# Shifted value blocks of streaming heads: built by SBUF-to-SBUF transfers on SyncE's queue instead of GpSimd copies, from the fourth chunk on

## The chip, the core and the metric

The kernel runs on one core of a Trainium2 chip. The core has five engines, each with its own in-order queue of instructions: TensorE (PE in the profile, its weight loads PEld), VectorE (DVE), ScalarE (ACT), GpSimd (POOL) and SyncE (SP). SyncE does no arithmetic here; it only begins transfers. Sixteen DMA engines move the data of all transfers, whoever begins them. The metric is the time of one execution on the device in microseconds (us), less being better; the time given for a kernel is the median of its runs.

## What is computed

Attention with two kinds of heads, followed by a gated feed-forward block. Four batches, 8 heads, 768 positions, 64 values per head. "Retrieval" heads (0, 2 and 6) see every earlier position; the other five, the "streaming" heads, see a window of the last 64 positions and the first 4 positions, the sinks.

```python
stream_keep = causal & (is_sink | in_win)      # is_sink: pos < 4, in_win: rel < 64
mask = np.where(retr[0, :, 0, 0, None, None], full_mask, stream_mask)
scores = np.where(mask[None, :, :, :], scores, -1000000000.0)
a = np.exp(scores - max)  ;  a = a / sum(a)
attn = np.matmul(a, v)
...
h = x @ w_in                                   # x: attn as 3072 x 512, w_in: 512 x 2048
g = h * (1.0 / (1.0 + np.exp(-beta * h)))
return (g @ w_out)                             # w_out: 2048 x 512
```

## The kernel before

**Units and chunks.** Each half sequence (384 positions, three blocks of 128) of a batch is a chunk; there are eight, c0 to c7, in the order (batch 0, first half), (1, first), (0, second), (1, second), (2, first), (3, first), (2, second), (3, second). A chunk has four units, one per pair of heads: heads (0, 2), (1, 3), (4, 6), (5, 7). So the first unit of a chunk has no streaming head, and the second has two. Units 0 to 7 (c0, c1) run in a hand-written start, `RAMP`. From unit 8 on, a loop with one turn `t` per unit (line 833) lays the scores of unit t, the value products of unit t-1 and slices of the feed-forward block of earlier chunks beside each other, in the order of a hand-written row of `PLAN`.

**Values.** `load_v` (line 124) brings a block of values from HBM by SP's queue into `vs`; `cast_v` (line 248) converts it to bf16 in `VX`, a buffer for each parity of the batch with six blocks of 128 positions by 8 heads by 65 numbers (64 values and a one, which makes the row sum). From c4 on GpSimd does this cast, for c2 and c3 VectorE.

**Shifted blocks.** A streaming head multiplies, for a block of queries, the block of keys before it as a whole. The first 64 of its 128 rows are outside every window, so rows 0 to 3 of that block are given to the sinks. The keys so rebuilt are `KO`, the values `VO`: four blocks per batch parity, copies of `VX` blocks 1 to 4 whose rows 0 to 3 are rows 0 to 3 of `VX` block 0. `sink_values(c)` (line 253) builds them: one block in a first half, three in a second half, a copy of 128 partitions by 512 numbers for each and then one copy on 4 partitions for the sink rows. All of it runs on GpSimd. `values_at` (line 265) calls it right behind the chunk's third `cast_v`.

**What follows from VO.** Value products (`steps_PV`, line 515) accumulate in PSUM in `po`; `normalize` (line 538) divides by the sum into `x`; `x_by_dma` (line 558) turns two units' `x` into half of `xT` by a DMA transpose on SP's queue. The feed-forward block of a chunk (line 600, then 653) needs both halves of its `xT`: of the four products of a 128-column slice, the first two read the half of the first two units, the third and fourth the other half.

**Other users of the queues.** GpSimd also begins the loads of rows of queries and keys from HBM (`load_rows`, line 276, 12 for each chunk). SP begins, besides `vs` and `xT`, the DMA transposes of those rows into `KT` and `QTD` (lines 294 and 297, six for each chunk) and the stores of results (line 659).

**What sets the order.** `later(delay, fn)` (line 73) keeps a function until a modelled clock, which each step of PE advances by its listed cost, has passed the time plus `delay`, or until someone who needs it calls it. Everything is issued in this order into the engines' queues, and dependencies between engines become semaphore waits.

```python
    def values_at(c, t, delay):
        def go():
            cast_v(c, t, nc.vector.tensor_copy if c < 4 else nc.gpsimd.tensor_copy)
            if t == HT - 1:
                sink_values(c)
        chunk_values.setdefault(c, []).append(later(delay, go))
```

Of the kernel before, what the change touches and what calls it, by code (L numbers as in the profile page):

```python
# [18 lines left out]
def kernel(  # L19
# [13 lines left out]
    nc = tc.nc  # L33
# [6 lines left out]
    HT = HALF // 128  # L40
    NPAIR = H // 2
    NU = B * 2 * NPAIR
# [3 lines left out]
    n_sink_i = 4  # L46
# [26 lines left out]
    def later(delay, fn):  # L73

        todo = [fn]

        def once():
            if todo:
                todo.pop()()
        heapq.heappush(heap, (clock[0] + delay, count[0], once))  # L80
        count[0] += 1
        return once
# [40 lines left out]
    def load_v(c, held=False, tiles=range(HT)):  # L123
        b, h2 = chunks[c]
        if tiles[0] == 0:
            staged["v", c] = stage.tile([128, HT, H, D], F32, name="vs")
        vs = staged["v", c]
        if held:
            nc.gpsimd.memset(vs[:, :, 0, 0:1], 0.0)
        for t in tiles:  # L130
            r = h2 * HALF + t * 128
            nc.sync.dma_start(out=vs[:, t], in_=v[b, :, r:r + 128, :].rearrange("h p d -> p h d"))  # L132
# [115 lines left out]
    def cast_v(c, t, copy):  # L248

        b, h2 = chunks[c]  # L250
        copy(out=VX[b % 2][:, h2 * HT + t, :, 0:D], in_=staged["v", c][:, t])  # L251

    def sink_values(c):
        b, h2 = chunks[c]
        ka, kz = (1, 2) if h2 == 0 else (2, 5)
        vx, vo = VX[b % 2], VO[b % 2]
        copy = nc.gpsimd.tensor_copy if c < 2 else nc.gpsimd.tensor_copy
        for i in range(ka, kz):
            copy(out=vo[:, i - 1, :, 0:D], in_=vx[:, i, :, 0:D])  # L259
        copy(out=vo[0:n_sink_i, ka - 1:kz - 1, :, 0:D],  # L260
             in_=vx[0:n_sink_i, 0:1, :, 0:D].to_broadcast([n_sink_i, kz - ka, H, D]))

    chunk_values = {2: []}

    def values_at(c, t, delay):
        def go():
            cast_v(c, t, nc.vector.tensor_copy if c < 4 else nc.gpsimd.tensor_copy)
            if t == HT - 1:
                sink_values(c)
        chunk_values.setdefault(c, []).append(later(delay, go))  # L270

    def sinks_at(u, delay):
        st_u[u]["sinks"] = later(delay, lambda: sinks_of(u))


    def load_rows(c):

        b, h2 = chunks[c]

        def rows(name, src, t, i):  # L280
            r = h2 * HALF + t * 128
            nc.gpsimd.dma_start(out=ROWS[c % 2, name][:, t, i * 4 * D:(i + 1) * 4 * D].rearrange("p (h d) -> p h d", d=D),  # L282
                                in_=src[b, i:H:2, r:r + 128, :].rearrange("h p d -> p h d"))
        return [lambda name=name, src=src, t=t, i=i: rows(name, src, t, i)
                for name, src in (("k", k), ("q", q)) for t in range(HT) for i in range(2)]

    def transposes_dma(c, names=("k", "q")):
        b, h2 = chunks[c]
        kr, qr = ROWS[c % 2, "k"], ROWS[c % 2, "q"]
        QT = QTD[(c + 1) % 2]  # L290
        for t in range(HT):
            j = h2 * HALF + t * 128
            if "k" in names:
                nc.sync.dma_start_transpose(out=KTB[b % 2][:, :, j:j + 128], in_=kr[:, t])
        for t in range(HT):
            if "q" in names:
                nc.sync.dma_start_transpose(out=QT[:, :, t * 128:(t + 1) * 128], in_=qr[:, t])
        for u in range(c * NPAIR, (c + 1) * NPAIR):
            p = u % NPAIR
            st_u[u] = {"QT": QT[:, place[p], :]}  # L300
# [34 lines left out]
    def steps_T(u):  # L335
        def go():
            transpose_qk(u, "k")
            transpose_qk(u, "q")
            copy_qk(u, "k", nc.vector.tensor_copy)
            copy_qk(u, "q", nc.scalar.copy)  # L340
            st_u[u]["sinks"] = later(600, lambda: sinks_of(u))
        return [(350, go)]
# [172 lines left out]
    def steps_PV(u):  # L515
        b, h2, p = units[u]
        s = st_u.setdefault(u, {})

        def head(hh, qi, last):
            def go():  # L520
                for f in s["masks"] + chunk_values[u // NPAIR] if u >= 8 else []:
                    f()
                if "po" not in s:
                    if u < 8 and u % 2:
                        po = ps_m.tile([128, 512], F32, name="mm")
                        s["po"] = po[:, 0:HT * 2 * (D + 1)].rearrange("p (t h d) -> p t h d", t=HT, h=2)
                    else:
                        s["po"] = sums_bank(u)[:, 0:HT * 2 * (D + 1)].rearrange("p (t h d) -> p t h d", t=HT, h=2)
                po = s["po"]
                lst = s["blocks"][hh][qi]  # L530
                for j, (e, val) in enumerate(lst):
                    nc.tensor.matmul(po[:, qi, hh, :], e, val, start=(j == 0), stop=(j == len(lst) - 1))  # L532
                if last and u >= 8:
                    normalize(u)
            return (len(s["blocks"][hh][qi]) * 38, go)
        return [head(hh, qi, hh == 1 and qi == HT - 1) for qi in range(HT) for hh in range(2)]
# [26 lines left out]
    def steps_X(g):  # L563

        def go():
            src = xg.pop(g)
            tp = ps_m.tile([128, 512], F32, name="mm").bitcast(BF16)[:, 0:2 * HALF].rearrange("p (a t j) -> p a t j", a=2, t=HT)
            for a in range(2):
                for t in range(HT):
                    nc.tensor.transpose(tp[:, a, t, :], src[:, a, t].rearrange("p h d -> p (h d)"), ident)  # L570
            x_tp[g] = tp
            if g >= 4:
                copy_x(g, nc.vector.tensor_copy)
        return [(340, go)]
# [111 lines left out]
    def run(steps):  # L686
        for x in steps:
            step(x)
# [8 lines left out]
    def do(word):  # L697
# [15 lines left out]
        elif what == "cv":  # L713
            cast_v(n, i, copies[eng])
        elif what == "vo":
            sink_values(n)
        elif what == "pv":
            pv = products.setdefault(n, [])
# [51 lines left out]
    def feed(x):  # L770

        a = done[0] < len(first) and all((first[done[0]][0], p) in avail for p in range(2))
        b = done[1] < len(second) and done[0] >= due[second[done[1]][0]]
        c = first[done[0]][0] if a else 0
        fresh = c > 1 and clock[0] < since[c] + 1300
        if b and (x == "b" or not a or fresh):
            done[1] += 1
            step(second[done[1] - 1][1])
        elif a:
            wide[0] = x == "A"  # L780
            done[0] += 1
            step(first[done[0] - 1][1])
            wide[0] = False
# [49 lines left out]
    for t in range(8, NU + 2):  # L833
        c, i = (t + 5) // NPAIR, (t + 5) % NPAIR
        if t >= 14 and c < NCHUNK and i < 3:
            for x, f in enumerate(load_rows(c)[4 * i:4 * i + 4]):
                later(1000 + 1500 * x, f)
        c, i = (t + 4) // NPAIR, (t + 4) % NPAIR
        if t >= 12 and c < NCHUNK and i < HT:
            later(2500, lambda c=c, i=i: load_v(c, tiles=[i]))  # L840
        c, i = (t + 3) // NPAIR, (t + 3) % NPAIR
        if t >= 9 and c < NCHUNK and i < HT:
            values_at(c, i, 3000)
        if t > 14 and t % NPAIR == 2 and t // NPAIR + 1 < NCHUNK:
            transposes_dma(t // NPAIR + 1)
        if 12 <= t + 1 < NU:
            sinks_at(t + 1, 1000)
        qk = steps_QK(t) if t < NU else []
        pv = steps_PV(t - 1) if 8 <= t - 1 < NU else []
        xx = steps_X(5) if t == 13 else steps_X(NU // 2 - 1) if t == NU + 1 else []  # L850
        tr = steps_T(t + 1) if t + 1 < 12 else []

        plan = PLAN[t - 8]
        for x in plan.split():
            if x == "V":
                run(qk[:1])
                qk = qk[1:]
            elif x == "p":
                run(pv[:1])
                pv = pv[1:]  # L860
            elif x == "T":
                run(tr)
                tr = []
            elif x == "X":
                run(xx)
                xx = []
            elif len(x) > 1:
                do(x)
            else:
                feed(x)  # L870
        run(qk + tr + xx + pv)
    i = 0
# [39 lines left out]
```

## Time and profile before

| | |
|---|---|
| time, median of 3 runs | 228.94 us (228.17 to 230.06) |
| time of the profiled execution | 228.94 us |
| its span, first to last instruction | 227.0 us |
| granted TensorE clock | 0.999 |
| VO copies on GpSimd, whole blocks (line 259) | 16, median 0.627 us |
| VO copies on GpSimd, sink rows (line 260) | 8, 0.607 to 1.679 us |
| value products that read VO (line 532) | 80 |
| share of the 16 DMA engines, 60 to 200 us: SP's queue (q1), GpSimd's queue (q0) | 52.4%, 41.6% |

The span is what the trace covers; the execution's time is 1.94 us longer. A row of a group of instructions reads: line, engine, operation, what is written and read, shape, count, then busy microseconds and mean nanoseconds of one, then the idle time of the engine before them and what ended it. A timeline row reads: start, duration, engine, line, operation, tiles, count, and the idle time before in brackets. For SP ("SPq") a row is the time in which the queue issues a transfer, not the transfer itself; how long that takes to land is told in the view of the transfers. On GpSimd the issue of a transfer is an instruction of its own (DMA_DIRECT2D, about 0.75 us).

### The profile page before, as it was taken

The page shows a single profiled execution, that of the slowest core. Times are in us where ns is not written, and L with a number is a line of the kernel's source. Part 1 is how long each engine was busy: PE and PEld are TensorE (multiplying, and loading weights), DVE is VectorE, ACT ScalarE, POOL GpSimd, SP SyncE. Part 2 cuts the span into 40 slices and gives each one's busy share as a digit, 9 for nine tenths or more (in the row PEclk, how much of TensorE's full clock was granted, in tenths as well). Part 3 has the DMA queues.
Part 4 walks back from the last instruction along what each step waited for, and adds up shares of the span by engine and source line. Part 5 has one row for each costly group of instructions (what it writes and reads, how often), then busy time and mean ns, then how long its engine had stood idle before and what let it go on. Part 6 is the DMA issues. An engine that isn't in the chain of part 4 may idle for free.

```text
span 227.0 us, 5019 instructions
## 1 busy us (share of the span) xinstructions
PE 219.4 (97%) x1898; PEld 126.4 (56%) x1917; DVE 142.1 (63%) x342; ACT 154.0 (68%) x254; POOL 87.3 (38%) x143
## 2 busy tenths in 40 slices
PE   7989999999999999999999999999999999999994
PEld 3555766654655665556654664556645655456553
DVE  4679888852684779357932699646963779028600
ACT  2698898946767897449933887569876878139621
POOL 5377952249163399143064049910670000000000
PEclk9999999999999999999999999999999999999999
DMA  6999999999999899989869779596963030111012
GB/s 204 262 301 239 225 197 198 195 220 171 149 216 178 161 153 144 141 175 133 103 131 162 126 151 140 92 133 103 216 64 107 24 81 0 49 46 46 0 49 92
DMA packets 95383, 31.66 MB, mean 139 GB/s; under 512 B 81776, under 2 KB 92416, under 8 KB 95360
## 3 DMA queue, kind: packets, MB, share of 16 engines
q1 hardware_dynamic: 58880, 22.82, 50.2%
q0 software_dynamic: 35904, 8.13, 41.9%
q10 hardware_dynamic: 576, 0.40, 0.6%
q8 instruction: 15, 0.25, 0.5%
q14 instruction: 8, 0.07, 0.1%
HBM read 27.27 MB, written 6.29 MB: 148 GB/s over the span
## 4 chain that ended last, share of the span: by engine, by line
PE 89%; DMA 4%; DVE 2%; SPq 2%; issue 1%; ACT 0%; ACTq 0%; DVEq 0%
PE mm L653 34%; PE mm L600 25%; PE sp L600 12%; PE sp L451 6%; PE po L532 6%; DMA s<-in_k_dram 3%; DMA s<-in_q_dram 2%; PE mm L638 2%; DVE es L478 1%; PE mm L322 1%; SPq L132 1%; PE mm L570 1%; PE mm L451 1%; SPq L119 1%; PE sp L422 1%
## 5 line engine op out<-in xcount | busy, mean ns | idle before, releaser
L653 PE MATMUL mm<-w_out_sb,gT 128*128 128x512 bf16 x349 | 84.1, 379 | 1.3 <-issue 0.5
L460 ACT ACTIVATE es<-sp 128x768 bf16<-128x768 f32 (+2 forms) x72 | 56.5, 837 | 19.6 <-PE sp L451 19.4
L600 PE MATMUL mm<-xT,w_in_sb 128*128 128x384 bf16 x348 | 64.6, 326 | 0.0
L600 PEld LDWEIGHTS <-w_in_sb 128*128 128x128 bf16 x512 | 47.8, 98 | 29.7 <-issue 0.2
L605 ACT ACTIVATE th<-mm,beta_h 128x384 f32<-128x384 f32 x87 | 49.8, 588 | 5.6 <-PE mm L600 0.9
L653 PEld LDWEIGHTS <-gT 128*128 128x128 bf16 x368 | 33.4, 98 | 36.0 <-issue 1.5
L608 DVE SCALAR_TENSOR_TENSOR gT<-th,mm 128x384 bf16<-128x384 f32 x87 | 46.8, 551 | 7.4 <-ACT th L605 3.8
L282 POOL DMA_DIRECT2D s<-in_q_dram x30 | 22.4, 761 | 27.2 <-DMA QTD<-s 21.7
L600 PE MATMUL sp<-xT,w_in_sb 128*128 128x384 bf16 x164 | 32.3, 326 | 0.0
L657 ACT ACTIVATE osb<-mm 128x512 f32<-128x512 f32 x23 | 13.8, 602 | 26.1 <-PE mm L653 25.8
L532 PEld LDWEIGHTS <-es 128*128 128x128 bf16 x472 | 23.3, 98 | 13.6 <-issue 1.5
L608 DVE SCALAR_TENSOR_TENSOR gT<-th,sp 128x384 bf16<-128x384 f32 x41 | 22.3, 552 | 5.6 <-ACT th L605 3.7
L532 PE MATMUL po<-VX,es 128*128 128x65 bf16 x360 | 24.9, 194 | 0.8 <-ACT VX L251 0.4
L605 ACT ACTIVATE th<-sp,beta_h 128x384 f32<-128x384 f32 x41 | 23.8, 586 | 2.3 <-PE sp L600 0.2
L282 POOL DMA_DIRECT2D s<-in_k_dram x30 | 22.4, 759 | 6.8 <-DMA w_out_sb<-in_moe_w_out_dram 5.2
L251 POOL CAST VX<-vs 128x512 bf16<-128x512 f32 x16 | 10.6, 662 | 34.6 <-DMA vs<-in_v_dram 31.8
L541 DVE RECIPROCAL rec<-po 128x6 f32<-128x6 f32 x28 | 5.4, 193 | 27.0 <-PE po L532 27.0
L478 DVE TENSOR_TENSOR es<-es,Mh 128x768 bf16<-128x768 bf16 (+1 forms) x26 | 17.4, 698 | 5.0 <-ACT es L460 4.4
L451 PE MATMUL sp<-QTD,KT 64*128 64x128 bf16 (+2 forms) x258 | 19.2, 240 | 0.6 <-ACT QTD L333 0.3
L545 DVE TENSOR_TENSOR x<-po,rec 128x384 bf16<-128x384 f32 x28 | 15.6, 557 | 1.0
L451 PEld LDWEIGHTS <-KT 64*128 64x128 bf16 x278 | 11.1, 94 | 5.8 <-issue 3.6
L259 POOL COPY VO<-VX 128x512 bf16<-128x512 bf16 x16 | 10.0, 649 | 7.3 <-DVE VX L251 7.3
(74 smaller groups left out, 157.2 us busy)
## 6 DMA issues: line engine op xcount, KB each, us to landing
vs<-in_v_dram SPq DMA_DIRECT2D x24, 256.0 KB, 5.5
out_dram<-osb SPq DMA_DIRECT2D x23, 256.0 KB, 2.8
w_in_sb<-in_moe_w_in_dram POOLq DMA_DIRECT2D x4, 512.0 KB, 9.7
w_out_sb<-in_moe_w_out_dram POOLq DMA_DIRECT2D x4, 512.0 KB, 16.5
s<-in_k_dram POOLq DMA_DIRECT2D x30, 64.0 KB, 4.8
s<-in_q_dram POOLq DMA_DIRECT2D x30, 64.0 KB, 5.1
s<-in_k_dram SPq DMA_DIRECT2D x4, 384.0 KB, 6.8
s<-in_q_dram SPq DMA_DIRECT2D x4, 384.0 KB, 8.6
```

The costliest lines, as they stand in the source:

```text
L251: copy(out=VX[b % 2][:, h2 * HT + t, :, 0:D], in_=staged["v", c][:, t])
L282: nc.gpsimd.dma_start(out=ROWS[c % 2, name][:, t, i * 4 * D:(i + 1) * 4 * D].rearrange("p (h d) -> p h d", d=D), in_=src[b, i:H:2, r:r + 1 ...
L451: nc.tensor.matmul(sps[i][r][:, x * 128:y * 128], key(a, lhs), s["QT"][half(a), qi * 128:(qi + y - x) * 128], start=first, stop=first or y ...
L460: nc.scalar.activation(out=views[i].rearrange("p r k j -> p r (k j)"), in_=banks[2][:, :, 0:n * 128], func=ACTF.Exp, scale=scale)
L478: nc.vector.tensor_mul(ev[:, :, 0:n], ev[:, :, 0:n], Mh[h2][:, None, m0:m0 + n].to_broadcast([128, 2, n, 128]))
L532: nc.tensor.matmul(po[:, qi, hh, :], e, val, start=(j == 0), stop=(j == len(lst) - 1))
L545: nc.vector.tensor_mul(xg[g][:, :, :, u % 2, :].rearrange("p a t d -> p t a d"), po[:, :, :, 0:D], rec.to_broadcast([128, HT, 2, D]))
L600: nc.tensor.matmul(hp[:, 0:HALF], w_in_sb[:, mo, fi * 128:(fi + 1) * 128], xT[c][:, mo, :], start=(mo == 0), stop=(mo == MO - 1))
L605: nc.scalar.activation(out=th, in_=hp[:, 0:HALF], func=ACTF.Tanh, scale=beta_h[:, fi:fi + 1])
L608: nc.vector.scalar_tensor_tensor(out=gTs[c][:, fi, :], in0=th, scalar=1.0, in1=hp[:, 0:HALF], op0=ALU.add, op1=ALU.mult)
L653: nc.tensor.matmul(op, gTs[c][:, fi, ns * 128:(ns + 1) * 128], w_out_sb[:, fi, :], start=(fi == 0), stop=(fi == FO - 1))
L657: nc.scalar.activation(out=osb, in_=op, func=ACTF.Copy, scale=0.5)
```

## The change

From the fourth chunk on (c3 to c7) `sink_values` begins transfers on SP's queue and returns, and GpSimd does no copies. One transfer copies partitions 4 to 127 of all the chunk's blocks (1 or 3 blocks, lying side by side, with the ones); then one transfer for each block copies the four sink rows. So it is 2 transfers for c4 and c5 and 4 for c3, c6 and c7: 16 in place of 16 copies (11 of whole blocks, 5 of sink rows). The call is taken out of `values_at` and gets a due time of its own: 2500 on the modelled clock after the beginning of the turn of the chunk's first unit. In SP's queue the transfers then stand

- c3: behind the first load of c4's values, ahead of a result's store
- c4: behind the first load of c5's values, ahead of the second `xT` transpose of c3
- c5: behind the first load of c6's values, ahead of a result's store
- c6: behind the first load of c7's values, ahead of the second `xT` transpose of c5
- c7: behind the first `xT` transpose of c6, ahead of a result's store

The order of instructions on PE, VectorE and ScalarE is the same in both kernels.

```diff
@@ sink_values
         vx, vo = VX[b % 2], VO[b % 2]
+        if c > 2:
+            nc.sync.dma_start(out=vo[n_sink_i:128, ka - 1:kz - 1], in_=vx[n_sink_i:128, ka:kz])
+            for i in range(ka, kz):
+                nc.sync.dma_start(out=vo[0:n_sink_i, i - 1], in_=vx[0:n_sink_i, 0])
+            return
         copy = nc.gpsimd.tensor_copy if c < 2 else nc.gpsimd.tensor_copy
@@ values_at
             cast_v(c, t, nc.vector.tensor_copy if c < 4 else nc.gpsimd.tensor_copy)
-            if t == HT - 1:
-                sink_values(c)
         chunk_values.setdefault(c, []).append(later(delay, go))
+
+    def sink_values_at(c, delay):
+        chunk_values.setdefault(c, []).append(later(delay, lambda: sink_values(c)))
@@ the loop over t
             values_at(c, i, 3000)
+        if 12 <= t < NU and t % NPAIR == 0:
+            sink_values_at(t // NPAIR, 2500)
```

## The prediction

> **What bounds the kernel now.** I read the engines' shares first, then the chain that ended last, then the engines' busy time in the stretch in which the changed steps lie (columns: stretch, its length, busy time of PE, PEld, DVE, ACT, POOL, the clock, the DMA engines' mean busy time, GB/s), then who waits on PE.
>
> ```profile
> PE 219.4 (97%) x1898; PEld 126.4 (56%) x1917; DVE 142.1 (63%) x342; ACT 154.0 (68%) x254; POOL 87.3 (38%) x143
> PE 89%; DMA 4%; DVE 2%; SPq 2%; issue 1%; ACT 0%; ACTq 0%; DVEq 0%
> 45.00:185.00 140.00, 138.48 (x1229) 78.78 (x1243) 89.79 (x230) 99.30 (x161) 62.52 (x86) 1.00 1.11 140
> PE po L532 <- DVE es L478: 0.4, 1, 0.4
> PEld L532 <- DVE es L478: 0.9, 1, 0.9
> ```
>
> PE bounds it, at full clock. POOL, which the change relieves, is busy 38% and not in the chain. From 45 to 185 us, which holds every step that changes, PE idles 140.00 - 138.48 = 1.52 us. So whatever is taken off another engine gives back at most 1.52 us, 0.7% of the time. A change of over 1% (2.29 us of 228.94; about what a measurement of this kernel can tell from no change) is possible to the slow side alone, by making PE wait where it doesn't now. The one wait in mid-kernel is in the last two rows: PE for a mask multiplication on DVE (line 478).
>
> **Removed: the GpSimd copies.** They explain that wait. First the multiplication in a stretch without VO copies beside it (100 to 130 us, of its own shape), then in the stretch of c6's copies, then GpSimd there.
>
> ```profile
> L478 DVE TENSOR_TENSOR es<-es,Mh 128x768 bf16<-128x768 bf16 x3 | 1.7, 555 | 0.3 <-ACT es L460 0.3
> ...
> L478 DVE TENSOR_TENSOR es<-es,Mh 128x768 bf16<-128x768 bf16 x1 | 2.6, 2553 | 0.0
> ...
> 139.90 1.75 POOL L259 COPY VO<-VX 128x512 bf16<-128x512 bf16 x3
> 141.71 1.68 POOL L260 COPY VO<-VX 4x1536 bf16<-4x1536 bf16 x1
> 143.34 2.97 POOL L282 DMA_DIRECT2D s<-in_k_dram  x4
> 146.27 2.27 POOL L282 DMA_DIRECT2D s<-in_q_dram  x3
> ```
>
> Beside the copies the multiplication took 2.553 us instead of 0.555: 2.0 us lost on DVE, of which 0.4 shows as a wait of the matmuls and 0.9 as one of the weight loads. The page "SBUF — State Buffer" of the Trainium skill, section "SBUF: two separate sides", says that VectorE and GpSimd share a pair of ports, held for a whole instruction while the other blocks; these rows agree. I put the gain at 0.5 us, between the 0.4 and the 0.9. The other copies cost PE nothing now: no wait of PE in the middle names them.
>
> The copies' 3.43 us (139.90 to 143.33) also stood ahead of seven loads of c7's rows in GpSimd's queue, which now begin 3.4 us earlier.
>
> **Added: 16 transfers, and what stands behind them.** They must land before the first value product that reads VO. SP's rows on either side of the new issues, then PE's first reads (c3, c4, c6, c7; c5 is as c4, with more room):
>
> ```profile
> 70.78 0.42 SPq L132 DMA_DIRECT2D vs<-in_v_dram  x1
> 75.87 0.34 SPq L659 DMA_DIRECT2D out_dram<-osb  x1
> ...
> 94.80 0.43 SPq L132 DMA_DIRECT2D vs<-in_v_dram  x1
> 97.13 1.22 SPq L560 DMA_TRANSPOSE xT<-x  x1
> ...
> 143.88 0.33 SPq L659 DMA_DIRECT2D out_dram<-osb  x1
> 144.30 0.39 SPq L132 DMA_DIRECT2D vs<-in_v_dram  x1
> 145.78 1.21 SPq L560 DMA_TRANSPOSE xT<-x  x1
> ...
> 161.66 1.88 SPq L560 DMA_TRANSPOSE xT<-x  x1
> 170.23 0.36 SPq L659 DMA_DIRECT2D out_dram<-osb  x1
> ```
>
> ```profile
> 80.69 0.19 PE L532 MATMUL po<-VO,es 128*128 128x65 bf16 x1
> ...
> 104.81 0.20 PE L532 MATMUL po<-VO,es 128*128 128x65 bf16 x1
> ...
> 154.59 0.19 PE L532 MATMUL po<-VO,es 128*128 128x65 bf16 x1
> ...
> 178.63 0.19 PE L532 MATMUL po<-VO,es 128*128 128x65 bf16 x1
> ```
>
> From issue to first read there are 80.69 - 71.20 = 9.5 us for c3, and in the same way 9.6, 9.9 and 15.1. An issue takes SP about 0.42 us (143.88 to 144.30), so four take 1.7 and two 0.8; the idle gaps of SP there are 4.7, 1.9, 1.1 and 6.7 us, each filled with waiting for an engine's result. Only at c6 do the issues overrun (by 0.6 us). The transfers wait for the casts that they copy. The tightest is c7's second (its third block isn't copied):
>
> ```profile
> 162.39 0.62 POOL L251 CAST VX<-vs 128x512 bf16<-128x512 f32 x1 [0.27 <-PE sp L600]
> ```
>
> It ends at 163.01, and SP arrives at 161.66 + 1.88 = 163.54, so no new wait stands in front of what is queued there.
>
> How long does a transfer take? No row shows one from SBUF to SBUF with plain rows. The nearest is a result's store by itself, in a window of 3.5 us (packets, megabytes, share of 16 engines; then the landing in us):
>
> ```profile
> q1 hardware_dynamic: 144, 0.26, 19.9%
> issues: line engine op xcount, KB each, median us to landing
> out_dram<-osb SPq DMA_DIRECT2D x1, 256.0 KB, 2.0
> ```
>
> The 144 packets are 128 rows and a closing one on each engine. 0.199 x 3.5 = 0.70 us on each engine for 8 rows of 2048 bytes, and 1.3 us of the 2.0 are fixed. A three-block transfer is 124 rows of 3120 bytes (3 x 8 x 65 x 2). Laid over 16 engines it is 8 rows at most, 24,960 bytes, 1.07 us. But 124 is not a multiple of 16, and if rows are dealt out evenly, as 128 rows are here, 4 is the largest count up to 16 that divides it: 31 rows, 96,720 bytes, 4.13 us on each of four engines, while twelve do nothing. The three sink transfers have four rows each, so they add 3120 bytes, 0.13 us, to at most four engines. I take the even split: 4.26 us for a three-block chunk (1.20 at the other end), as the trace has no uneven one. The page "DMA: Bandwidth & Descriptors" of the Trainium skill, section "Why a DMA increments its semaphore by 16 and not by 1", has the same rule for transfers begun by SP and ACT (100 partitions run on 10 engines); no run here shows it yet.
>
> Even at 4.26 us the values land 5.6 us after their issue (1.3 fixed), and with half of each engine given to other queues after 9.8, at c3 and c6 just at the first read. What is queued *behind* them on those four engines is nearer to its deadline. At c6 that is the second half of c5's `xT`. Its landing, from the issues of 145 to 147 us, beside the landings of all ten such transposes; PE's products, in the timeline and in the chain; and the engines from 142 to 144 us:
>
> ```profile
> xT<-x SPq DMA_TRANSPOSE x1, 7.2
> ...
> DMA to landing us min/median/max: 2.7/5.1/7.2
> ...
> 153.29 1.46 PE L600 MATMUL mm<-xT,w_in_sb 128*128 128x384 bf16 x8
> ...
> 153.46 1.30 PE mm L600 x8
> ...
> 142.00:144.00 2.00, 1.88 (x14) 0.89 (x14) 2.00 (x4) 1.15 (x2) 2.00 (x2) 1.00 0.04 1
> ```
>
> It lands at 145.78 + 7.2 = 152.98. The third product, the first that reads it, starts two products of 0.163 us (1.30 us for eight in the chain) after 153.29, at 153.62: a slack of 0.64. Two things change relative to PE, which itself comes 0.5 us earlier. The transfer puts 4.26 us ahead of it. The seven loads, which share the engines with it now (7.2 us, the longest of the ten, where the shortest is 2.7), begin 3.4 us earlier, in a stretch where the DMA engines are idle (0.04 of 2.00), so 2.9 earlier relative to PE. If that all comes back, `xT` lands 4.26 - 2.9 = 1.4 us later and PE waits 0.7.
>
> The sum: 228.94 (the profiled execution's time, which is also the median) - 0.5 + 0.7 = **229.1 us**.
>
> Other moves: c3's copies hold five loads of rows until 66.17; without them these go out behind the load before the copies, from 56.2 us on, while c3's own transposes land. The load before, the five, the last two transposes with the landing of the second, PE's read, the engines from 64 to 68 us, and the loads' queue in a window of 2 us:
>
> ```profile
> 55.46 0.78 POOL L282 DMA_DIRECT2D s<-in_k_dram  x1
> ...
> 66.17 3.71 POOL L282 DMA_DIRECT2D s<-in_k_dram  x5
> ...
> 62.65 2.52 SPq L297 DMA_TRANSPOSE QTD<-s  x2
> ...
> QTD<-s SPq DMA_TRANSPOSE x1, 2.7
> ...
> 70.03 0.34 PE L451 MATMUL sp<-QTD,KT 64*128 64x384 bf16 x2
> ...
> 64.00:68.00 4.00, 3.95 (x24) 1.75 (x25) 3.10 (x9) 3.19 (x5) 3.87 (x5) 1.00 0.92 229
> ...
> q0 software_dynamic: 895, 0.11, 87.5%
> ```
>
> The last transpose is issued at 64.0 and lands at 66.7: 3.3 us of room. A load's 64 KB are 512 packets of 128 bytes, 32 on an engine, at 0.875 x 2 x 16 / 895 = 0.031 us: 1.0 us, five of them 5.0, so at most 1.7 us of wait. I take none, since the DMA engines are idle for 3.1 of the 4 us from 64 to 68. c4's and c5's transfers are one block (1.4 us on four engines), c7's has nothing due soon behind it.
>
> **The rivals.** *Hidden altogether* (0.27): the transfers run on all engines, or the freed loads clear the way entirely. 1.20 - 2.9 is below zero, `xT` isn't late, and the removed wait is all: 228.4. For it speaks that every row of the trace uses all 16 engines.
>
> *`xT` stuck behind the transfer* (0.23), the other side: four engines, and the earlier loads do not help, because packets of the two queues alternate and as many loads' packets are left when `xT`'s turn comes. Then 4.26 - 0.64 = 3.6 us of wait, 228.94 - 0.5 + 3.6 = 232.0. It becomes a loss of over 1% once the transfer's net delay of `xT` passes 0.64 + 0.5 + 2.29 = 3.4 us. For it speaks the 7.2 us that this very transpose takes beside the loads, against it the idle stretch before.
>
> *Values late* (0.05): few or one engine. All 124 rows on one would take 124 x 3120 bytes at the store's rate, 16.5 us, against 9.5 at c3: about 8 us lost there and 13 more at c6, near 250. Nothing in the trace points to it.
>
> **How the numbers follow.** The forecast of 229.1 has a chance of 0.45. Range: from "hidden" less 0.5 us (the fastest run shown lies 0.8 under the median) to the stuck `xT` plus 0.2: 227.9 to 232.2. It leaves out the late values and some of the stuck case with the 1.7 us of the early loads. Its own cases: forecast and "hidden" lie within 1% (0.72), the stuck `xT` and the late values beyond (0.28, of which I count 0.04 back within, for a partial wait). Faster by over 1% would need more than all of PE's idle time: 0.02, for the measurement, taken from "hidden". That makes 0.74 within 1% and 0.24 slower.
>
> **What would show it.** In the changed profile: line 478 back at 555 ns throughout and no wait of PE on it (the gain); GpSimd's seven loads from about 139.9 us; the transfers' landing after issue, near 3 us (16 engines) or 5.6 and more (four); the wait, if any, at the first slice of c5's feed-forward products near 153.5 us, with `xT` as its releaser, or at a first product with VO. I would be wrong if PE waited anywhere else, such as for `QTD` near 70 us.

## The result and the profile after

| | us |
|---|---|
| changed kernel, median of 6 runs | 231.43 (230.91 to 232.5) |
| kernel before, median of 6 runs beside them | 228.94 (228.17 to 230.06) |
| ratio, with its 95% interval | 1.0113 (1.0084 to 1.0143) |
| profiled execution of the changed kernel: time, span, clock | 232.5, 230.8, 0.993 |

The change costs 2.5 us, 1.1%. Ratios, here and in the experiments, leave out the few executions that took over 1.5% longer than the fastest of their kernel; medians and ranges hold all of them. The lines of the changed kernel lie six further on (L606 is the first feed-forward product, before L600; L484 the mask multiplication, before L478). First the engines' shares, SP's queue q1 (packets, megabytes, share) and the chain of work, then q1 before the change:

```profile
PE 222.0 (96%) x1898; PEld 127.5 (55%) x1917; DVE 138.0 (60%) x342; ACT 154.3 (67%) x254; POOL 74.3 (32%) x127
...
q1 hardware_dynamic: 59608, 24.28, 51.3%
...
PE 90%; DMA 6%; ACT 1%; issue 1%; DVE 1%; POOL 0%; ACTq 0%
```

```profile
q1 hardware_dynamic: 58880, 22.82, 50.2%
```

GpSimd lost 13 us of work and DVE 4. Neither weighs on the path: GpSimd had no part in the chain before, DVE 2%. The next answers are the list of PE's waits, PE's timeline at the first slice of c5's feed-forward, and the chain that ends there:

```profile
PE mm L606 <- DMA xT<-x: 2.1, 1, 2.1
```

```profile
153.26 0.49 PE L606 MATMUL mm<-xT,w_in_sb 128*128 128x384 bf16 x2
155.80 1.22 PE L606 MATMUL mm<-xT,w_in_sb 128*128 128x384 bf16 x6 [2.05 <-DMA xT<-x]
```

```profile
149.10 6.66 DMA xT<-x
155.76 0.04 issue
155.80 1.22 PE mm L606 x6
```

In the profile of before all eight products ran in one piece from 153.29. Now two run, and the third waits 2.05 us for the second half of `xT`, which lands at 155.76 instead of 152.9. The next views show why it starts late, in SP's queue and in GpSimd's:

```profile
143.85 0.33 SPq L665 DMA_DIRECT2D out_dram<-osb  x1
144.27 0.39 SPq L132 DMA_DIRECT2D vs<-in_v_dram  x1
144.75 0.66 SPq L258 DMA_DIRECT2D VO<-VX  x1
145.47 3.54 SPq L260 DMA_DIRECT2D VO<-VX  x3
149.10 1.32 SPq L566 DMA_TRANSPOSE xT<-x  x1
```

```profile
140.48 2.99 POOL L288 DMA_DIRECT2D s<-in_k_dram  x4
143.41 2.29 POOL L288 DMA_DIRECT2D s<-in_q_dram  x3
```

The four issues of c6 took 149.10 - 144.75 = 4.35 us, and `xT` was issued 149.10 - 145.78 = 3.3 us later than before. GpSimd's seven loads began at 140.48, 2.9 us earlier. The prediction had 3.4 by the clock and 2.9 relative to PE; PE came to the first product at the same time as before (153.26 and 153.29), so the 2.9 holds. The mask multiplication beside c6's old copies, by shape, from 138 to 146 us:

```profile
L484 DVE TENSOR_TENSOR es<-es,Mh 128x768 bf16<-128x768 bf16 x1 | 1.0, 981 | 0.0
L484 DVE TENSOR_TENSOR es<-es,Mh 128x512 bf16<-128x512 bf16 x1 | 0.4, 413 | 0.0
```

It fell from 2.553 us, and PE's wait on it is gone. It is not back at the 0.555 that the prediction named, although no copies stand beside it.

**What the profiled execution adds.** It is the slowest of the six, 1.07 us above their median. The rows of two microseconds behind the wait give the reason (the clock is the third value from the end):

```profile
154.00:156.00 2.00, 0.20 (x2) 0.13 (x2) 0.36 (x1) 0.60 (x2) 0.00 (x0) 1.00 0.90 170
156.00:158.00 2.00, 2.00 (x14) 1.12 (x13) 0.89 (x2) 1.16 (x2) 0.00 (x0) 0.68 0.95 141
158.00:160.00 2.00, 2.00 (x11) 1.12 (x10) 0.78 (x2) 0.63 (x2) 0.00 (x0) 0.50 0.51 70
160.00:162.00 2.00, 2.00 (x16) 1.15 (x14) 1.11 (x2) 1.57 (x3) 1.01 (x2) 0.96 0.39 78
```

PE ran at a granted clock of 0.5 for about (1.28 + 2.00 + 0.16) = 3.4 us. Compared product by product with the trace of before, PE loses 2.25 us at the wait and another 1.62 in these 3.4. The other five runs show a mean clock of 0.999 to 1.000, so they can't have paid the second part.

**Four engines, counted.** Before, q1 had 58880 packets; after, 59608, 728 more. The sixteen transfers have 664 rows (3 x 124 in c3, c6 and c7, 2 x 124 in c4 and c5, and four sink rows for each of 11 blocks). That leaves 64 closing packets, four for each transfer: every one of them ran on four engines. So the rule that the prediction named from the page "DMA: Bandwidth & Descriptors" of the Trainium skill, section "Why a DMA increments its semaphore by 16 and not by 1", agrees with this trace for transfers within SBUF.

By the trace's record of each packet, the 124 packets of 3120 bytes of c6 took 20.5 us in all, so 5.1 us on each of four engines, against the 4.13 reckoned, and stretched from 147.63 to 154.27. So the values were there 9.5 us after the issue at 144.75, the prediction's crowded case (9.8) and not its 5.6; before, the first product with c6's VO stood at 154.59. The values were all but late as well.

### The profile page after: what moved, and what is told of

Its sections match the earlier page's. It is cut to its first block, busy times and chain, and to the rows that moved or that the text cites. A ratio compares the mean times of both kernels' runs of the same rounds, so it can differ in the third digit from the quotient of the medians.

```text
span 230.8 us, 5028 instructions
## 1 busy us (share of the span) xinstructions
PE 222.0 (96%) x1898; PEld 127.5 (55%) x1917; DVE 138.0 (60%) x342; ACT 154.3 (67%) x254; POOL 74.3 (32%) x127
## 3 DMA queue, kind: packets, MB, share of 16 engines
q1 hardware_dynamic: 59608, 24.28, 51.3%
## 4 chain that ended last, share of the span: by engine, by line
PE 90%; DMA 6%; ACT 1%; issue 1%; DVE 1%; POOL 0%; ACTq 0%
PE mm L659 32%; PE mm L606 24%; PE sp L606 12%; PE sp L457 6%; PE po L538 6%; DMA w_in_sb<-in_moe_w_in_dram 3%; DMA xT<-x 3%; PE mm L167 2%; PE mm L328 2%; PE mm L644 2%; PE po L519 1%; PE sp L428 1%; PE mm L576 1%; PE mm L457 1%; PE mm L538 0%
## 5 line engine op out<-in xcount | busy, mean ns | idle before, releaser
L606 PE MATMUL mm<-xT,w_in_sb 128*128 128x384 bf16 x348 | 65.7, 329 | 2.1 <-DMA xT<-x 2.1
L606 PEld LDWEIGHTS <-w_in_sb 128*128 128x128 bf16 x512 | 48.1, 98 | 32.9 <-issue 3.3
L606 PE MATMUL sp<-xT,w_in_sb 128*128 128x384 bf16 x164 | 32.9, 331 | 0.2 <-DMA w_in_sb<-in_moe_w_in_dram 0.2
L538 PEld LDWEIGHTS <-es 128*128 128x128 bf16 x472 | 23.8, 98 | 13.2 <-issue 1.8
L251 POOL CAST VX<-vs 128x512 bf16<-128x512 f32 x16 | 10.1, 631 | 45.0 <-DMA vs<-in_v_dram 38.7
L484 DVE TENSOR_TENSOR es<-es,Mh 128x768 bf16<-128x768 bf16 (+1 forms) x26 | 14.2, 573 | 5.2 <-ACT es L466 4.6
L538 PE MATMUL po<-VO,es 128*128 128x65 bf16 x72 | 11.1, 198 | 0.0
```

The source lines that it names most:

```text
L484: nc.vector.tensor_mul(ev[:, :, 0:n], ev[:, :, 0:n], Mh[h2][:, None, m0:m0 + n].to_broadcast([128, 2, n, 128]))
L606: nc.tensor.matmul(hp[:, 0:HALF], w_in_sb[:, mo, fi * 128:(fi + 1) * 128], xT[c][:, mo, :], start=(mo == 0), stop=(mo == MO - 1))
```

## The experiments

All are made from the changed kernel or the one before. "Wait at c5" is the wait of PE for `xT` in the first slice of c5's feed-forward. The kernel before was run anew beside each group of them, on the same chip: median 228.50 us beside e1, e2, e4 and e5, 228.55 beside e3, e6, e7 and e8, 228.58 beside e9 to e12. Waits are those of the one profiled execution of each kernel.

**Sixteen engines (e1_sixteen).** The large transfer in two, 112 rows and 12.

```diff
-            nc.sync.dma_start(out=vo[n_sink_i:128, ka - 1:kz - 1], in_=vx[n_sink_i:128, ka:kz])
+            for p0, p1 in ((16, 128), (n_sink_i, 16)):
+                nc.sync.dma_start(out=vo[p0:p1, ka - 1:kz - 1], in_=vx[p0:p1, ka:kz])
```

> The changed kernel with its large transfer cut in two: rows 16 to 127 (112 rows, 7 on each of sixteen engines if dealt out evenly) and rows 4 to 15 (12 rows on twelve engines), so one issue more on SP for each chunk, the same bytes. Theory A (3120-byte rows of c6 stand 31 deep on four engines ahead of the second xT transpose of c5): the wait of PE for xT of about 2.1 us goes, xT lands within 0.7 us of 153 us, time 228.5 to 229.3. Rival B (it is SP's issues that make xT late: 149.1 us instead of 145.8 us, so the number of transfers counts): one issue more makes it no better, PE waits 2 us or more, time 231.4 or above.

Measured: 229.44 us, ratio 1.0019 (0.9979 to 1.0059). The wait at c5 is gone, as theory A has it (the time is 0.1 us above its range), although there is one issue more ahead of `xT`; rival B wanted 231.4. But the profile has two other waits, from the list of PE's waits between 60 and 160 us:

```profile
PE sp L458 <- DMA QTD<-s: 1.4, 1, 1.4
PE mm L607 <- DMA xT<-x: 0.8, 1, 0.8
```

The first begins at 69.9 us, before the first transfer of VO is issued at 71.0; the second, near 127 us, is at c4's feed-forward.

**c6 alone by copies (e2_c6_copies).** GpSimd builds c6's blocks at the old place, all others go by transfers.

```diff
-        if c > 2:
+        if c in (3, 4, 5, 7):
@@ values_at, behind cast_v
+            if t == HT - 1 and c not in (3, 4, 5, 7):
+                sink_values(c)
@@ the loop over t
-        if 12 <= t < NU and t % NPAIR == 0:
+        if t < NU and t % NPAIR == 0 and t // NPAIR in (3, 4, 5, 7):
```

> The changed kernel with c6 alone given back to GpSimd's copies, at their old place; c3, c4, c5 and c7 by transfers. If the loss lies at c6 alone, PE shows the wait for the mask multiplication near 141 us again (0.4 to 0.9 us), none for xT, and the time is that of before, 228.7 to 229.3. If the other chunks' transfers cost something too (rival D), the time lies over 229.5.

Measured: 229.81 us, 1.0051 (1.0011 to 1.0092). No wait at c5, but one of 1.1 us for c4's `QTD` near 95 us. So c6 isn't the whole of the loss: the other chunks' transfers by themselves cost 0.5% (0.1 to 0.9%), as rival D has it. The mask wait was absent here too, though the copies were back beside the multiplication: that contradicted the prediction's first term and led to the second trace below.

**c6's transfers earlier (e4_c6_early).** Behind the first `xT` transpose of c5 instead of ahead of the second.

```diff
-        if 12 <= t < NU and t % NPAIR == 0:
+        if 12 <= t < NU and t % NPAIR == 0 and t != 24:
             sink_values_at(t // NPAIR, 2500)
+        if t == 23:
+            sink_values_at(6, 1000)
```

> The changed kernel with c6's transfers moved up in SP's queue alone: directly behind the first xT transpose of c5 (near 136 us), where SP then waits some 7 us for a result of ScalarE, instead of behind the load of values at 144 us. The same transfers on the same engines. Theory A: they are done before the second xT transpose is issued, PE waits for neither, the mask's wait is gone as well: 228.2 to 228.9, the fastest so far. If PE waits for xT all the same, it is not the order in the queue: 231 or above.

Measured: 231.54 us, 1.0114 (1.0067 to 1.0161). The waits of PE:

```profile
PE mm L606 <- DMA xT<-x: 2.3, 1, 2.3
PE sp L606 <- DMA xT<-x: 0.6, 1, 0.6
```

Now the large transfer was issued at 137.56, but its packets ran from 139.76 to 148.07 among GpSimd's loads, and the four engines were still behind when `xT` came: issued at 146.47, it took 10.24 us to land. So the place that I thought was free wasn't: moved up here, the transfers met the loads. Three of the four runs took 231.4 to 231.8 us; why the fourth took 229.33 no trace shows.

**c6's blocks left out (e5_c6_left_out).** The kernel before, but nobody builds c6's VO.

```diff
@@ sink_values, in the kernel before
+        if c in (6,):
+            return
@@ values_at, behind cast_v
-            if t == HT - 1:
+            if t == HT - 1 and c not in (6,):
                 sink_values(c)
```

> The kernel before with c6's shifted value blocks left out altogether (VO keeps the values of c2; the other chunks by GpSimd's copies as before). It holds the gain alone, and the earlier begin of the seven loads of rows, without any transfer. Theory A: PE's wait for the mask goes, xT lands before 153.6 us: 0.4 to 0.6 us under the kernel before, 228.3 to 228.6. Rival C (the loads that come earlier delay xT): PE waits for xT near 153 us and the time is above the kernel before.

Measured: 228.48 us, 1.0006 (0.9991 to 1.0022). So building c6's blocks costs the kernel before nothing that the medians show (0.1% at most): theory A's gain of 0.4 to 0.6 us isn't there. Rival C falls: no wait appears. It also gives the relief by itself: GpSimd's loads, the issue of `xT`, the first products, and the time that `xT` took to land:

```profile
141.17 2.98 POOL L287 DMA_DIRECT2D s<-in_k_dram  x4
```

```profile
146.45 1.21 SPq L565 DMA_TRANSPOSE xT<-x  x1
```

```profile
153.97 1.46 PE L605 MATMUL mm<-xT,w_in_sb 128*128 128x384 bf16 x8
```

```profile
xT<-x SPq DMA_TRANSPOSE x1, 4.4
```

It lands 153.97 - 146.45 - 4.40 = 3.12 us ahead of the first product. The mask multiplication took 0.955 us here, with no copies of c6 at all, so the 0.555 of the quiet stretch wasn't what it would fall to.

**c6 alone by transfers (e3_c6_only).**

```diff
-        if c > 2:
+        if c in (6,):
@@ values_at, behind cast_v
+            if t == HT - 1 and c not in (6,):
+                sink_values(c)
@@ the loop over t
-        if 12 <= t < NU and t % NPAIR == 0:
+        if t < NU and t % NPAIR == 0 and t // NPAIR in (6,):
```

> Only c6's blocks are put together by transfers (as in the changed kernel: 124 rows in one transfer, then three for the sinks); all other chunks' by GpSimd's copies. Theory A (the transfers of one three-block chunk put some 4 us on four DMA engines, and what shares those engines in the stretch from 140 to 156 us lands late): the wait for c5's xT at the first slice of its feed-forward is there by itself, 2.0 to 2.5 us, the mask wait of 0.5 is gone, and no other wait appears (none for QTD near 70 or 95 us, none for xT of c3 or c4): 228.5 + 1.7 = 230.2 us, up to 0.5 more for the beginning. Rival C (the wait at c5 is summed up from all chunks, each of which leaves its queues a little later): under 1 us of wait, 229 us.

Measured: 230.40 us, 1.0102 (1.0057 to 1.0147), the 230.2 of theory A. The wait at c5 is there by itself and no other appears; rival C falls. c6 alone thus costs nearly what all chunks together do (1.0113). Whether the other chunks' 0.5% of e2 adds to it in full can't be told within these intervals. In its profiled execution, 3 us slower than the other three, the wait was longer than the theory's 2.0 to 2.5 us, and the clock was again at half speed behind it:

```profile
152.48 0.49 PE L608 MATMUL mm<-xT,w_in_sb 128*128 128x384 bf16 x2
156.74 1.14 PE L608 MATMUL mm<-xT,w_in_sb 128*128 128x384 bf16 x6 [3.77 <-DMA xT<-x]
```

**c6 alone, on sixteen engines (e6_c6_sixteen).** Both edits together, that of e1 and that of e3.

> Only c6's blocks by transfers, and the large one cut into rows 16 to 127 (112 rows, dealt to 16 engines) and rows 4 to 15; all other chunks by GpSimd's copies. Theory A: 7 rows of 3120 bytes on each engine, about 1 us, so c5's xT is not late for its reader although SP issues it some 2 us later; the mask wait of 0.5 us goes and nothing takes its place: 228.0 us, between 227.5 and 228.5, the least of all kernels so far. Rival B (five issues ahead of xT in SP's queue, 0.6 to 0.85 us each, are what makes it late): a wait of 1 us or more at c5's first slice, 229.5 us.

Measured: 228.22 us, 0.9978 (0.9953 to 1.0003). First SP's queue, then PE at c5:

```profile
144.79 1.75 SPq L259 DMA_DIRECT2D VO<-VX  x2
146.60 1.91 SPq L261 DMA_DIRECT2D VO<-VX  x3
148.62 1.25 SPq L569 DMA_TRANSPOSE xT<-x  x1
```

```profile
153.30 1.46 PE L609 MATMUL mm<-xT,w_in_sb 128*128 128x384 bf16 x8
```

`xT` is issued at 148.62, 0.5 us earlier than in the changed kernel and 2.8 later than before, yet it lands after 4.58 us instead of 6.66, 0.10 us ahead of the first product where the changed kernel is 2.50 behind it, and the eight products run in one piece. So the four engines were worth 2.6 us of `xT`'s delay. The transfers aren't free on sixteen either: against e5's 3.12, `xT` lands 3.0 us later relative to the first product, and it was issued 2.8 later (4.68 us ahead of that product instead of 7.52). It is still in time: these 3.0 us are less than the 3.12 of e5. The same 124 rows of 3120 bytes took 1.1 us on each of sixteen engines (17.3 us in all). SP's queue q1:

```profile
q1 hardware_dynamic: 59056, 23.22, 49.6%
```

That is 176 packets more than before: 136 rows and 40 closings, 16 for the 112 rows, 12 for the 12 and four for each sink transfer. Theory A is borne out; rival B wanted 229.5. The interval reaches 1.0003, so a gain over the kernel before isn't shown.

**c3 by copies, c4 to c7 on sixteen engines (e7_c3_copies_16).** e1 with `if c in (4, 5, 6, 7)`.

> c4 to c7 by transfers with the large one cut for sixteen engines, c3 by GpSimd's copies as in the kernel before, which hold back five loads of rows until 66 us. Theory D (the wait for c3's QTD near 70 us, 1.4 us in the kernel with all chunks on sixteen engines, comes from these five loads, which then go out beside c3's own transposes): no wait for QTD near 70 us; what is left is a wait of up to 1 us for c4's xT near 127 us, and the mask wait is gone: 228.5 us. Rival E (that wait changes from execution to execution and has nothing to do with c3's copies): a wait for QTD of over 0.5 us near 70 us here too, or none in any kernel again.

Measured: 228.42 us, 0.9991 (0.9975 to 1.0007), and its list of PE's waits names none after the kernel's beginning. That fits theory D: c3's move would cost about 1 us of the 229.44 of e1. But the two intervals overlap, and the changed kernel, e2, e4, e8 and e9 begin the same loads early and have no wait near 70 us, so it isn't shown.

**c3 both ways (e12_c3_both).** e1, and GpSimd makes c3's copies as well, into a buffer `VS` at the old place.

```diff
@@ values_at, behind cast_v
+            if t == HT - 1 and c == 3:
+                vx = VX[1]
+                for i in range(2, 5):
+                    nc.gpsimd.tensor_copy(out=VS[:, i - 2, :, 0:D], in_=vx[:, i, :, 0:D])
+                nc.gpsimd.tensor_copy(out=VS[0:n_sink_i, 0:3, :, 0:D],
+                                      in_=vx[0:n_sink_i, 0:1, :, 0:D].to_broadcast([n_sink_i, 3, H, D]))
```

> All chunks from c3 on by transfers, cut for sixteen engines, and beside it GpSimd makes c3's copies at their old place into a buffer that nobody reads, so that the five loads behind them begin at 66 us as in the kernel before. With these copies and without c3's transfers the median was 228.42, without the copies and with the transfers 229.44. Theory D (the loads that begin earlier delay c3's QTD): no wait for QTD near 70 us, 228.5 us, and a narrow spread (under 2 us). Rival H (c3's transfers themselves cost it): 229.4 us, as without the copies.

Measured: 228.78 us, 0.9995 (0.9965 to 1.0024), and the runs that the ratio counts lie between 227.6 and 230.2. No wait near 70 us, but 1.4 us for `xT` at c4's feed-forward near 130. The median lies between D's 228.5 and H's 229.4, and the spread isn't narrow. What c3's part costs is left open: between nothing and 1 us, and not the same in every execution.

**No relief (e8_both).** The changed kernel, and GpSimd makes c6's copies too, into a buffer that nobody reads.

```diff
@@ values_at, behind cast_v
+            if t == HT - 1 and c == 6:
+                b, h2 = chunks[c]
+                ka, kz = (1, 2) if h2 == 0 else (2, 5)
+                for i in range(ka, kz):
+                    nc.gpsimd.tensor_copy(out=VS[:, 0, :, 0:D], in_=VX[b % 2][:, i, :, 0:D])
+                    nc.gpsimd.tensor_copy(out=VS[0:n_sink_i, 0, :, 0:D], in_=VX[b % 2][0:n_sink_i, 0, :, 0:D])
```

> The changed kernel, and beside it GpSimd makes the copies of c6's blocks too, at their old place, into a buffer that nobody reads (three of 128 rows, three of the four sink rows). So the seven loads behind them begin as late as in the kernel before, and the transfers stay. It takes away the relief that the prediction set at 2.9 us. Theory A1 (the relief is there, about 2.1 us, as xT landed that much earlier where c6 was left out): c5's xT lands about 158 us, PE waits 4 us for it at c5's first slice, the mask wait of 0.4 us is back: 233 us. Rival A2 (the earlier loads free nothing, since packets of the queues alternate): the landing stays near 156 us, the wait 1.7 to 2.2 us, and with the mask wait the time is 231.0 to 231.5 us.

Measured: 237.94 us, 1.0375 (1.0327 to 1.0422), more than either theory gave. GpSimd's loads, then PE at c5:

```profile
145.56 2.97 POOL L295 DMA_DIRECT2D s<-in_k_dram  x4
148.49 2.28 POOL L295 DMA_DIRECT2D s<-in_q_dram  x3
```

```profile
154.02 0.49 PE L613 MATMUL mm<-xT,w_in_sb 128*128 128x384 bf16 x2
160.78 2.08 PE L613 MATMUL mm<-xT,w_in_sb 128*128 128x384 bf16 x6 [6.27 <-DMA xT<-x]
```

Against the changed kernel, and counted from the first of the eight products, the loads begin (154.02 - 145.56) = 8.46 us ahead instead of (153.26 - 140.48) = 12.78, so 4.3 us later; and PE waits 6.27 instead of 2.05, 4.2 longer. In this pair the relief is real, and nearly one for one; rival A2, with a wait of 2.2 at most, falls. The loads came later than I had meant, since six short copies take longer than three and one; that, and the half clock that follows (6.8 us of it in the profile, and a mean clock of 0.985 to 0.986 in all four timed runs), fits a time above 233. The mask wait that theory A1 expected back is not there, although the copies are.

**One sink transfer in place of three (e9_one_sink).** Two issues fewer, the same bytes.

```diff
-            for i in range(ka, kz):
-                nc.sync.dma_start(out=vo[0:n_sink_i, i - 1], in_=vx[0:n_sink_i, 0])
+            nc.sync.dma_start(out=vo[0:n_sink_i, ka - 1:kz - 1],
+                              in_=vx[0:n_sink_i, 0:1].to_broadcast([n_sink_i, kz - ka, H, D + 1]))
```

> The changed kernel with one transfer for the sink rows of all of a chunk's blocks in place of three (the same bytes, the same four engines): two issues fewer at c3, c6 and c7. At c6 the second and third sink issue took 1.59 and 1.26 us on SP, and xT was issued 3.3 us later than in the kernel before. Theory A (the four engines' bytes delay xT; SP's issues only wait for room because those engines are behind): the wait for xT at c5's first slice stays between 1.7 and 2.3 us, 231 us. Rival B (the place behind the issues delays it, each issue 0.6 us and more by itself): xT lands 1.2 to 2.8 us earlier, the wait is between 0 and 0.9 us, 229.5 us.

Measured: 231.51 us, 1.0104 (1.0055 to 1.0153), the time of the changed kernel. SP and PE:

```profile
147.92 3.48 SPq L566 DMA_TRANSPOSE xT<-x  x1
```

```profile
154.74 0.49 PE L606 MATMUL mm<-xT,w_in_sb 128*128 128x384 bf16 x2
156.66 1.14 PE L606 MATMUL mm<-xT,w_in_sb 128*128 128x384 bf16 x6 [1.43 <-DMA xT<-x]
```

Counted from the first product, `xT` was issued 154.74 - 147.92 = 6.8 us ahead instead of 153.26 - 149.10 = 4.2, so 2.7 us earlier, but the wait shrank only by 0.6, and the issue itself now took 3.48 us instead of 1.32. The wait of 1.43 lies between the two theories' ranges, nearer to A. The large transfer's packets took 18.0 us in all here, 4.5 on each engine instead of 5.1: that alone is the 0.6. So with four engines behind, an earlier issue brings nothing; that the time on SP's sinks was SP waiting for room in their queues is inferred, no row names it. This profile has another wait, 1.3 us for c4's `QTD` near 96 us.

**c6, sixteen engines, one sink transfer (e10_c6_best).** e6 with the edit of e9.

> c6 alone by transfers, the large one cut into rows 16 to 127 and 4 to 15, the sinks in one: three issues; all other chunks by GpSimd's copies. Both theories: no wait for xT at c5's first slice, xT lands about 1 us before its reader needs it (0.4 us before with five issues), no other new wait. 228.1 us, a ratio of about 0.998; not below 227.8, since the whole gain is the mask wait of 0.5 us.

Measured: 228.50 us, 0.9994 (0.9972 to 1.0016); no wait at c5. No better than e6, and neither can be told from the kernel before.

**The kernel before, once more (e11_before_again).** Unchanged, for a second trace.

> The kernel before once more, for a second trace of it. The gain of the change was taken from a mask multiplication of 2.553 us beside c6's copies, while in two kernels that keep copies at that place beside transfers elsewhere (three to six copies) it took no longer than 1.7 us and no matmul waited for it. Theory F (what the multiplication loses beside the copies depends on how their beginnings fall together, so the gain is not there in every execution): the multiplication takes another time, and the wait of PE on it may be gone. Rival G (it is the same each time): 2.5 us and a wait of 0.4 again.

One run, 228.37 us. The mask multiplication by shape, from 138 to 146 us, and GpSimd's copies:

```profile
L478 DVE TENSOR_TENSOR es<-es,Mh 128x512 bf16<-128x512 bf16 x1 | 0.8, 830 | 0.0
L478 DVE TENSOR_TENSOR es<-es,Mh 128x768 bf16<-128x768 bf16 x1 | 0.6, 551 | 0.0
```

```profile
139.49 0.99 POOL L251 CAST VX<-vs 128x512 bf16<-128x512 f32 x1
140.44 1.92 POOL L259 COPY VO<-VX 128x512 bf16<-128x512 bf16 x3
```

The two multiplications began at 139.47 and took 1.30 us together, not 4.15. In the first trace they began at 139.51 and the copies at 139.90; here GpSimd's cast fell beside the first of them and was itself stretched to 0.99 us (0.65 before), so the copies began at 140.44, when the multiplications were nearly done. No matmul waited. Theory F holds. The execution is 0.57 us faster than the first profiled one. Until here it was 0.04 us ahead of it, and from the first product of c5 on (152.72 instead of 153.29) it is 0.57 ahead: the wait was worth 0.53 us. GpSimd's loads and that product:

```profile
143.82 2.97 POOL L282 DMA_DIRECT2D s<-in_k_dram  x4
```

```profile
152.72 1.46 PE L600 MATMUL mm<-xT,w_in_sb 128*128 128x384 bf16 x8
```

## Why the prediction was right, and where not

The measured 231.43 lies in the range of 227.9 to 232.2, and the wait is at the place that the prediction named as the likely one: the first slice of c5's feed-forward, with the second half of `xT` as its releaser, because 124 rows go to four engines. So the mechanism was right. The likeliest time, 229.1, was 2.3 us too low, and the range holds the result because it was stretched to the rival's 232.0. Of its chances, 0.74 stood on a time within 1%, but the median is 1.13% slower (interval 0.84 to 1.43%), on the side that had 0.24. PE's wait came between the forecast's 0.7 us and the 3.6 of the rival "`xT` stuck", at 2.05. With 2.05 for 0.7 the prediction's sum gives 230.5, still within 1%: what carried it beyond is something that the sum doesn't hold (see below), so the place in the range is in part luck. By its steps:

- **The even split on four engines**: right, shown by the packet counts, and by e1, e6, e7, e10 and e12, which have no wait at c5, against the changed kernel, e3, e4, e8 and e9, which all have one. The rival "hidden altogether" falls by it, and e6 shows what that rival would have been.
- **"The transfer puts 4.26 us ahead of it"**: this is the term of the sum that was mis-sized. Take the changed kernel against e5, whose loads begin equally early (12.78 and 12.80 us ahead of the first product): `xT` lands 155.76 - 153.26 = 2.50 us behind that product instead of 153.97 - 146.45 - 4.40 = 3.12 ahead. The transfers cost 5.6 us, 1.4 more than reckoned. The packets took 5.1 us on each engine instead of 4.13, which would explain 1.0; I took their duration from a store by itself, and here they shared the engines with the loads, which may be why. But by e6 2.6 of the 5.6 go with the four engines, and 3.0 are left on sixteen, where the sum would have put 1.20; there the later issue of `xT` (2.8 us) is about as large. How the two overlap on four engines isn't measured. Put 5.6 for 4.26 in the prediction's sum, and its `xT` is 2.7 us late and PE waits 2.1: the measured wait.
- **The relief of 2.9 us**: there, and nearly one for one beside the transfers (e8 against the changed kernel: 4.3 us for the loads, 4.2 for the wait). The rival "stuck", which denied it, falls by this, though its time of 232.0 was nearer. Without transfers its size depends on the trace: from the first of before to e5 the loads begin 2.9 us earlier and `xT` lands 2.8 earlier, all relative to the first product; from the second (e11) the loads begin 3.9 earlier and `xT` lands only 1.2 earlier.
- **The issues "overrun only at c6, by 0.6"**: wrong as a number, and left out of the sum. They took 4.35 us instead of 1.7, and `xT` was issued 3.3 later. With four engines behind, that is not a delay to add: in e9 an issue 2.7 us earlier gave 0.6. On sixteen it looks like one: in e6 five issues make `xT` 2.8 later at its issue and 3.0 at its landing, against e5, and the relief hides it. But in e10, with three issues, `xT` goes out 1.1 us earlier than in e6, relative to the first product, and lands only 0.3 earlier, so its size is open.
- **The gain of 0.5**: right for the execution that was profiled (0.53 by e11), and in no later trace is that wait back, not in e2 and e8 either, where GpSimd copies c6's blocks. But it isn't a property of the kernel before: in its second trace the wait wasn't there either, and e5, which leaves the whole of c6's work out, gives 1.0006. So the median had little of it to give back.
- **The slack of 0.64 us**: also one execution's. In the second trace of before `xT` is issued at 145.20 and lands 5.57 later at 150.77, 1.95 us ahead of the first product at 152.72, where the first trace has 0.36. A forecast to a few tenths was not to be had from one trace.
- **c3's early loads and the other chunks at nothing**: the reason given was a misreading. The last column but one of the stretches is a share of the sixteen engines, and not a time: 0.92 from 64 to 68 us means that the engines were 92% busy (q1 79.6%, q0 12.1%), and not idle for 3.1 of the 4 us. (So with the 1.11 of the first view; the 0.04 from 142 to 144 us does say idle.) The bound of 1.7 us had nothing against it. The result is right for the profiled execution, which has no such wait, wrong over many: e2, where only these transfers are left, is 0.5% slower (0.1 to 0.9%), and e1, e2, e4, e8, e9 and e12 have waits of 0.6 to 1.4 us for `QTD` or `xT` of c3 and c4. At which of them PE waits changes from kernel to kernel; these runs don't settle why. On sixteen engines and without c3 (e7) none is left.

The sum with what was measured, in the two profiled executions: 228.94 - 0.53 for the mask wait + 2.25 for the wait at c5 is 230.7, 0.8 us under the median of 231.43. The changed kernel's execution was already 0.50 us late when that multiplication began (140.01 instead of 139.51); 0.34 of it was there at 34 us, before anything that changed. By medians, c6 alone costs 1.85 us (e3) and the whole change 2.49, and the 0.64 between them lies within what e2 gives the other chunks. How the median divides further is not measured.

## What to carry to other kernels

Count on how many engines a transfer will run before calling it small: 124 rows took 5.1 us on each of four engines, and the same bytes, cut as 112 and 12, took 1.1 on each of sixteen, and the wait was gone. Price such a transfer by what is queued behind it on those engines and due soon, not by its own reader, and don't expect one figure for a packet: c6's 124 packets on four engines took between 18.0 us (e9) and 24.4 (e8) in all. Count the issues as well: with the engines keeping up, five of them (e6) went with a landing 3.0 us later behind them. Look up what a column counts before leaning on it: a share read as a time made a busy stretch look idle. Before spending on a gain of half a microsecond that rests on one wait in one trace, take a second trace: here the wait wasn't there.

## What the runs showed of the hardware

**The clock dropped after a short wait.** In the changed kernel PE stood still for 2.05 us, and soon after it resumed ran at half clock for about 3.4 us. The page "TensorE: Matmul & The Clock Gate" of the Trainium skill, Part 1, says that the clock falls after a whole idle window of about 3.4 us. The length of the slow stretch agrees with that window; the wait before it was shorter. It doesn't happen each time: after the 2.28 us of e4 the clock stayed at 1.00, after the 3.77 of e3 it fell for 3.4 us and after the 6.27 of e8 for 6.8. These runs don't settle when it falls.

**A transpose behind four late engines is late.** `xT` took 6.66 us to land in the changed kernel and 9.3 in e8, behind transfers on four engines, 4.58 in e6, behind the same bytes on sixteen, and 4.4 in e5, with nothing ahead. That it is spread over all engines and waits for the last of them is inferred; no row names the engine of a packet.

**What two engines cost each other hangs on when they meet.** The same pair of multiplications cost DVE 4.15 us where GpSimd's copies began 0.4 us behind it and 1.30 where they began 1.0 behind it, when it was nearly done. Beside copies in e2 and e8 the pair took 2.06 and 1.68 us; without any, in e5, 1.29.
